# On-chip decay tables and a reordered opening in an attention, feed-forward and expert kernel

## The chip, the cores and the metric

The kernel runs on one core of one Trainium2 chip. The metric is the device time of one execution in microseconds (us). Three runs of the kernel before took 464.21, 465.52 and 466.25 us, with a median of 465.52 us. The engines are TensorE (PE in the profile; PEld is its weight load), VectorE (DVE), ScalarE (ACT), GpSimd (POOL) and SyncE (SP, which here only starts transfers). Each engine works off its own instructions in order and waits on semaphores.

## The reference, cut to what matters

Three steps follow one another: a linear attention with decay, a feed-forward layer, and a routed expert layer. The change touches the attention and the routing.

```python
# attention: 2 batches, 8 heads, 768 positions, head dim 64, blocks of 64; lam is one decay per head
Dmask = where(rel >= 0, lam ** rel, 0.0)              # rel = i - j inside a block
for b in range(nb):
    intra = (qb @ kb.T * Dmask) @ vb
    inter = (qb * lam ** (pos + 1)) @ kv_state        # query powers
    out[:, :, sl] = intra + inter
    kb_dec = kb * lam ** (block - 1 - pos)            # key decays
    kv_state = lam ** block * kv_state + kb_dec.T @ vb
# feed-forward on x = out as (1536, 512): w_in (512, 2048), w_out (2048, 512)
g = where(h > 0, h, exp(min(h, 0)) - 1) with h = x @ w_in;  x = g @ w_out
# experts: rows with x @ w_skip > 0 go to the expert with the largest x @ w_gate
y = gate * (relu(x @ w1[e]) @ w2[e]);  out = x + y on those rows
```

## The kernel before

The 1536 tokens are 12 chunks of 128 (the kernel takes attention blocks of 128, with decay powers to match), six chunks to a batch (CPS) and three to a token block (CPB). For a chunk `c` the attention steps are: `at_scores` (key-query products into two PSUM banks), `at_mask` (VectorE multiplies them by the table `mask`), `at_pv` (TensorE multiplies by the values), `at_qd` (GpSimd multiplies the queries by the power table `lp`), `at_inter` (TensorE adds queries times `state`), `at_kdec` (GpSimd multiplies the keys by the last column of `mask`), `at_kv` (key-value products), `at_decay` (GpSimd scales `state`) and `at_state` (VectorE adds the new products). `at_evac_hi` and `at_evac_lo` split the result from PSUM into a high and a low part, `xT`, for products in three passes.

The tables come from `lam` by way of memory: VectorE makes the powers of each head in `z8` (8 rows), a transfer writes them to `z_dr` in device memory, and transfers from there spread them: `mask` with overlapping rows, and `lp` in two halves. These transfers stand in SP's queue ahead of the keys and values of chunks 0 to 2.

The feed-forward layer has 16 slices `f` of the weights. They arrive as 64-bit floats in 1 MB transfers (`load_ff`), which ScalarE and VectorE convert: `conv_v`, three integer steps `conv_bits`, `conv_hi` (ScalarE) and `conv_lo` (VectorE). `ff1_mm`, `ff1_act`, `ff1_elu`, `ff1_lo` and `ff2` are the layer for one slice and one token block; `LAG` (3) such steps run mixed with chunks 3 to 5, and after them the steps run two ahead. The order of all instructions from the first products on is the order in which the code is written (`manual_schedule`); every engine takes its own share of that order.

At the start ten dummy products of `warm` stand between the scores of chunks 0 to 2, after the first four. Later, `route_pick` and `route_send` of each chunk are put into the steps by the dictionaries `A` (after `ff1_mm`) and `B` (between the second and third `ff2`). `route_rank` is a small product of counts, and `route_send` calls it together with what follows from it.

## Time and profile before

| what | value |
| --- | --- |
| median of three runs | 465.52 us |
| the profiled execution's own time | 463.39 us |
| its span, first to last instruction | 461.3 us |
| TensorE busy | 444.2 us, 96% of the span |
| VectorE busy | 293.1 us, 64% |
| ScalarE busy | 235.2 us, 51% |
| GpSimd busy | 82.8 us, 18% |

The shares are means over stages with different limits. The profiled execution has 2.09 us outside its span. Times within a row count from the start of the span. Where a row ends in brackets, the engine was idle for that long before it, and the name behind the arrow is what ended the wait. A busy TensorE is one with matmuls in flight; it is not by that alone at its fastest.

### The profile page before, as it was taken

To read this page: it belongs to the slowest core of one execution; us is meant where nothing else is said; L and a number is where in the kernel's file an instruction comes from. 1 tells how busy PE (TensorE), PEld (TensorE's weight loads), DVE (VectorE), ACT (ScalarE), POOL (GpSimd) and SP (SyncE) were. 2 spreads that over 40 slices of the span, in tenths; PEclk is the share of its full clock that TensorE was granted. 3 is DMA by queue.
4 is the path that set the end of the run, shared out by engine and by line. 5 is a ranking of instruction groups with operands and counts; after the bars stand their busy time and mean duration, and the time that the engine had idled before them with its cause. 6 is when DMAs were issued, how large, how long until landed. Compare 5 with 4: busy or idle time off the path is not lost.

```text
span 461.3 us, 6824 instructions
## 1 busy us (share of the span) xinstructions
PE 444.2 (96%) x2596; PEld 389.6 (84%) x2596; DVE 293.1 (64%) x558; ACT 235.2 (51%) x378; POOL 82.8 (18%) x106
## 2 busy tenths in 40 slices
PE   8698999999999999999999999999999999999993
PEld 7587899899988888998888898899989788888882
DVE  3789999999622365345244223775546688999970
ACT  2234576776444322443233335465652688888850
POOL 1654002020100124102232000220002112222101
PEclk9999999999999999999999999999999999999998
DMA  6999994604101212210020006334338689999400
GB/s 246 394 416 409 319 123 89 264 1 143 40 1 68 93 35 92 91 70 23 11 91 1 1 0 251 115 105 165 132 136 308 213 313 395 364 366 372 185 18 34
DMA packets 26650, 74.91 MB, mean 162 GB/s; under 512 B 4050, under 2 KB 9690, under 8 KB 24560
## 3 DMA queue, kind: packets, MB, share of 16 engines
q1 hardware_dynamic: 24576, 69.26, 42.4%
q0 software_dynamic: 1600, 3.03, 1.7%
q10 hardware_dynamic: 432, 2.10, 1.2%
q8 instruction: 22, 0.36, 0.3%
q14 instruction: 20, 0.16, 0.1%
HBM read 66.09 MB, written 10.51 MB: 166 GB/s over the span
## 4 chain that ended last, share of the span: by engine, by line
PE 81%; issue 6%; POOL 4%; DVE 4%; DMA 2%; ACT 1%; SPq 0%; POOLq 0%; ACTq 0%; DVEq 0%
PE h L352 28%; PE y L388 21%; PE h L892 8%; PE aux L388 7%; PE y L917 6%; POOL state L314 1%; PE aux L443 1%; DMA lp<-z_dr 1%; PE aux L903 1%; PE aux L280 1%; PE aux L428 1%; PE aux L269 1%; PE y L269 1%; DVE wa L113 1%; DMA z_dr<-z 1%
## 5 line engine op out<-in xcount | busy, mean ns | idle before, releaser
L352 PE MATMUL h<-xT,wa 128*128 128x384 f32 x480 | 91.1, 338 | 1.2 <-DVE xT L293 1.2
L352 PEld LDWEIGHTS h<-xT,wa 128*128 128x128 f32 x480 | 84.7, 188 | 4.7 <-DVE xT L293 1.4
L388 PE MATMUL y<-wa,g 128*128 128x512 f32 x270 | 70.2, 400 | 0.0
L367 ACT ACTIVATE g<-e 128x384 fp32r<-128x384 f32 x64 | 33.4, 523 | 53.4 <-DVE e L364 53.3
L358 ACT ACTIVATE e<-h 128x384 f32<-128x384 f32 x64 | 31.2, 488 | 56.5 <-PE h L352 56.4
L364 DVE SCALAR_TENSOR_TENSOR e<-e,h 128x384 f32<-128x384 f32 x64 | 35.1, 548 | 34.1 <-ACT e L359 34.1
L388 PEld LDWEIGHTS y<-wa,g 128*128 128x128 f32 x270 | 49.0, 188 | 8.9
L352 PE MATMUL h<-xT,wb 128*128 128x384 f32 x288 | 54.2, 336 | 0.0
L352 PEld LDWEIGHTS h<-xT,wb 128*128 128x128 f32 x288 | 50.9, 188 | 2.0
L372 DVE TENSOR_TENSOR g<-e,g 128x384 fp32r<-128x384 f32 x64 | 37.3, 582 | 16.0 <-ACT g L367 16.0
L388 PE MATMUL y<-wb,g 128*128 128x512 f32 x162 | 40.3, 394 | 0.0
L523 POOL DMA_INDIRECT xe<-x,idx x12 | 12.2, 1015 | 148.8 <-DVE xgT L420 49.8
L892 PE MATMUL h<-wa,xgT 128*128 128x512 f32 x144 | 36.1, 397 | 0.1
L388 PEld LDWEIGHTS y<-wb,g 128*128 128x128 f32 x162 | 30.1, 188 | 5.5
L359 ACT ACTIVATE e<-e 128x384 f32<-128x384 f32 x64 | 33.6, 526 | 2.0
L892 PEld LDWEIGHTS h<-wa,xgT 128*128 128x128 f32 x144 | 26.5, 188 | 5.7 <-ACT xgT L419 0.3
L113 DVE TENSOR_TENSOR wa<-big,wa 128x1024 fp32r<-128x1024 f32 x22 | 26.6, 1234 | 4.3 <-ACT wa L112 4.1
L917 PE MATMUL y<-wa,ht 128*128 128x512 f32 x96 | 23.8, 398 | 0.0
L113 DVE TENSOR_TENSOR wa<-ahead,wa 128x1024 fp32r<-128x1024 f32 x18 | 21.6, 1246 | 2.9 <-ACT wa L112 2.7
L112 ACT ACTIVATE wa<-big 128x1024 fp32r<-128x1024 f32 x22 | 22.4, 1056 | 1.2 <-DMA big<-in_wex_dram 1.2
L388 PE MATMUL aux<-wa,g 128*128 128x512 f32 x90 | 23.0, 399 | 0.0
L926 POOL TENSOR_TENSOR o<-o,xg 128x512 f32<-128x512 f32 x7 | 9.1, 1299 | 71.4 <-ACT o L925 71.4
(199 smaller groups left out, 687.4 us busy)
## 6 DMA issues: line engine op xcount, KB each, us to landing
big<-in_wex_dram SPq DMA_DIRECT2D x17, 1024.0 KB, 5.8
ahead<-in_wex_dram SPq DMA_DIRECT2D x15, 1024.0 KB, 6.9
wb<-in_wff_dram SPq DMA_DIRECT2D x10, 1024.0 KB, 13.0
big<-in_wff_dram SPq DMA_DIRECT2D x5, 1024.0 KB, 7.3
big<-in_kq_dram SPq DMA_DIRECT2D x6, 512.0 KB, 3.2
big<-in_kv_dram SPq DMA_DIRECT2D x6, 512.0 KB, 4.2
out_dram<-x SPq DMA_DIRECT2D x12, 256.0 KB, 2.2
xg<-xe SPq DMA_DIRECT2D x8, 257.0 KB, 5.4
```

Of the source, the lines that this page charges most:

```text
L112: nc.scalar.activation(out=w[:, 0, cs], in_=src, func=ACTF.Copy)
L113: nc.vector.tensor_tensor(out=w[:, 1, cs], in0=src, in1=w[:, 0, cs].bitcast(F32), op=ALU.subtract)
L352: nc.tensor.matmul(out=h, lhsT=w[:, wi, k * P:(k + 1) * P], rhs=xT[b][:, xi, k, :], start=(k == 0 and i == 0), stop=(k == 3 and i == 2))
L358: nc.scalar.activation(out=e, in_=h, func=ACTF.Relu, scale=-1.0)
L359: nc.scalar.activation(out=e, in_=e, func=ACTF.Exp, scale=-1.0)
L364: nc.vector.scalar_tensor_tensor(out=e, in0=e, scalar=-1.0, in1=h_t.pop(n), op0=ALU.add, op1=ALU.max)
L367: nc.scalar.activation(out=g[:, 0, :], in_=e, func=ACTF.Copy)
L372: nc.vector.tensor_tensor(out=g[:, 1, :], in0=e_t.pop(n), in1=g[:, 0, :].bitcast(F32), op=ALU.subtract)
L388: nc.tensor.matmul(out=y_t[b, t], lhsT=g[:, gi, t * P:(t + 1) * P], rhs=w[:, wi, 512:1024], start=(f == 0 and i == 0), stop=(f == NF - 1 a ...
L523: sc = nc.gpsimd.indirect_dma_start(out=xe[:, :], out_offset=bass.IndirectOffsetOnAxis(ap=idx[:, c:c + 1], axis=0), in_=x2[:, :], in_offse ...
L892: nc.tensor.matmul(out=h, lhsT=xgT_t[e][:, xi, k * P:(k + 1) * P], rhs=w_t[NF + 8 * e + k][:, wi, j * 512:(j + 1) * 512], start=(i == 0), ...
L917: nc.tensor.matmul(out=y, lhsT=ht[:, hi, k, :], rhs=w_t[NF + 8 * e + 4 + k // 2][:, wi, (k % 2) * 512:(k % 2) * 512 + 512], start=(i == 0) ...
```

## The change

Key decays and query powers no longer come from device memory. TensorE transposes `z8` into a bank that VectorE copies to a new small table `kd` (128 by 8), and multiplies `z8` by a selection matrix `sel` (8 rows of zeros and ones, made by GpSimd) into a bank that ScalarE copies to `lp`. `mask` still goes by way of `z_dr`. The ScalarE queue starts five transfers where it started three. In the opening, the scores of chunk 2, the state of chunk 0 (now copied by ScalarE) and the state product of chunk 1 are written in another order, and ten of the fourteen dummy products go. `at_kv` makes eight products of 64 by 64 in two column halves of the array where it made four of 128 by 128. The first `ff1_mm` takes its products by pass and not by slice. `route_rank` moves behind the third `ff2`, `route_slot` to the step after, `route_send` one step later.

```diff
     gates = const.tile([P, NCH, 2], F32, name="gates")
     mask = mid.tile([P, H, P], F32, name="mask")
     lp = mid.tile([P, 4, P], F32, name="lp")
+    kd = mid.tile([P, H, 1], F32, name="kd")
     state = mid.tile([P, 4, P], F32, name="state")
 
     raw_q = {}
...
         if c % CPS != CPS - 1:
             k3 = kv_t[c][:, 0, :].rearrange("p (h d) -> p h d", h=H)
             nc.gpsimd.tensor_tensor(
-                out=k3, in0=k3, in1=mask[:, :, P - 1:P].to_broadcast([P, H, D]), op=ALU.mult
+                out=k3, in0=k3, in1=kd.to_broadcast([P, H, D]), op=ALU.mult
             )
...
     def at_pv(c, b=None):
-        o = b if b is not None else aux()
-        o_t[c] = o
+        first = c not in o_t
+        if first:
+            o_t[c] = b if b is not None else aux()
+        o = o_t[c]
         v = kv_t[c]
         for hp in range(4):
             cs = slice(hp * P, (hp + 1) * P)
...
                 h = 2 * hp + j
                 nc.tensor.matmul(
                     out=o[64 * j:64 * j + 64, cs], lhsT=v[:, 1, h * D:(h + 1) * D],
-                    rhs=pm_t[c, j][:, hp, :], start=(hp == 0), stop=(c % CPS == 0),
+                    rhs=pm_t[c, j][:, hp, :], start=(first and hp == 0),
+                    stop=(not first or c % CPS == 0),
                     skip_group_check=True,
...
 
-    def at_inter(c):
+    def at_inter(c, b=None):
         if c % CPS:
             qd = qd_t.pop(c)
+            first = c not in o_t
+            if first:
+                o_t[c] = b if b is not None else aux()
             for hp in range(4):
                 nc.tensor.matmul(out=o_t[c][:, hp * P:(hp + 1) * P], lhsT=state[:, hp, :],
-                                 rhs=qd[:, hp, :], start=False, stop=True, skip_group_check=True)
+                                 rhs=qd[:, hp, :], start=(first and hp == 0), stop=not first,
+                                 skip_group_check=True)
 
     def at_evac_hi(c):
         b, cc = divmod(c, CPB)
...
             return
         s = aux()
         t = kv_t[c]
-        for hp in range(4):
-            cs = slice(hp * P, (hp + 1) * P)
-            nc.tensor.matmul(out=s[:, cs], lhsT=t[:, 0, cs], rhs=t[:, 1, cs],
-                             start=True, stop=True)
+        for h in range(H):
+            r = slice(64 * (h % 2), 64 * (h % 2) + 64)
+            cs = slice(h * D, (h + 1) * D)
+            nc.tensor.matmul(out=s[r, cs], lhsT=t[:, 0, cs], rhs=t[:, 1, cs],
+                             start=True, stop=True, skip_group_check=True)
         s_t[c] = s.rearrange("p (k e) -> p k e", k=4)
 
     def at_decay(c):
...
         s3 = s_t.pop(c)
         for j in range(2):
             r = slice(64 * j, 64 * j + 64)
-            if c % CPS == 0:
+            if c == 0:
+                nc.scalar.activation(out=state[r, :, r], in_=s3[r, :, r], func=ACTF.Copy)
+            elif c % CPS == 0:
                 nc.vector.tensor_copy(out=state[r, :, r], in_=s3[r, :, r])
             else:
                 nc.vector.tensor_tensor(out=state[r, :, r], in0=s3[r, :, r],
...
         b, f = where(n)
         h = bank("h", 2)[:, 0:TB]
         w = w_t[f]
-        for k in range(4):
-            for i, (wi, xi) in enumerate(PASSES):
-                nc.tensor.matmul(out=h, lhsT=w[:, wi, k * P:(k + 1) * P], rhs=xT[b][:, xi, k, :],
-                                 start=(k == 0 and i == 0), stop=(k == 3 and i == 2))
+        turns = [(k, i) for k in range(4) for i in range(3)]
+        if n == 0:
+            turns = [(k, i) for i in range(3) for k in range(4)]
+        for j, (k, i) in enumerate(turns):
+            wi, xi = PASSES[i]
+            nc.tensor.matmul(out=h, lhsT=w[:, wi, k * P:(k + 1) * P], rhs=xT[b][:, xi, k, :],
+                             start=(j == 0), stop=(j == 11))
         h_t[n] = h
     def ff1_act(n):
         h = h_t[n]
...
     oh_t = {}
 
     def route_send(c):
-        route_rank(c)
-        route_exp(c)
-        route_slot(c)
         route_gate(c)
         route_out(c)
 
...
         alloc_chunk(1)
         alloc_chunk(2)
         z8 = ph[0].tile([H, ZW], F32, tag="v", name="z8", bufs=2)
+        sel = t2()[0:H]
         nc.sync.dma_start(out=z8[:, P + 1:P + 2], in_=lam.rearrange("(h o) -> h o", o=1))
+        load_ff(0, nc.scalar)
+        dma_kv(0, nc.scalar)
         dma_kq(0, nc.scalar)
-        load_ff(0, nc.scalar)
         dma_kq(1, nc.scalar)
+        dma_kv(1, nc.scalar)
         nc.vector.memset(z8[:, 0:P], 0.0)
         nc.vector.memset(z8[:, P:P + 1], 1.0)
         nc.vector.memset(zrow, 0.0)
+        nc.gpsimd.memset(sel, 0.0)
+        nc.gpsimd.affine_select(out=sel.rearrange("h k (j i) -> h k j i", j=2),
+                                in_=sel.rearrange("h k (j i) -> h k j i", j=2),
+                                pattern=[[-2, 4], [-1, 2], [0, 64]], compare_op=ALU.not_equal,
+                                fill=1.0, base=0, channel_multiplier=1)
+        make_identity(nc, ident)
         nc.gpsimd.memset(blank1[:, 0:1], 0.0)
         nc.gpsimd.memset(blank1[:, 1:2], 4096.0)
         n = 1
...
         with tc.issue_after(zw.ins):
             mr = nc.sync.dma_start(out=mask, in_=toep)
         with tc.issue_after(mr.ins):
-            dma_kv(0)
-            for j in range(2):
-                rows = bass.AP(tensor=zt.tensor, offset=zt.offset + j * ZW + P + 1,
-                               ap=[[0, 64], [2 * ZW, 4], [1, P]])
-                nc.sync.dma_start(out=lp[64 * j:64 * j + 64], in_=rows)
             dma_kq(2)
-            for c in range(1, CPB):
-                dma_kv(c)
+            dma_kv(2)
             load_ff(1)
             for c in range(CPB, CPS):
                 alloc_chunk(c)
...
                 dma_kv(c)
                 load_ff(c - 1)
 
-        make_identity(nc, ident)
         nc.gpsimd.memset(ones, 1.0)
         nc.gpsimd.affine_select(out=ustrict, in_=ones, pattern=[[1, P]], compare_op=ALU.is_gt,
                                 fill=0.0, base=0, channel_multiplier=-1)
...
                 nc.tensor.matmul(out=b[:, 0:P], lhsT=zrow[:, 0:P], rhs=zrow[:, 0:P],
                                  start=True, stop=True)
 
-        sb = [[bank("h", 2), bank("h", 2)], [bank("y", 3), bank("y", 3)],
-              [bank("y", 3), aux()]]
+        sb = [[bank("h", 2), bank("h", 2)], [bank("y", 3), bank("y", 3)]]
         warm(sb[0][0], WARM[0])
+        lpb, kdb = aux(), aux()
+        nc.tensor.transpose(out=kdb[:, 0:H], in_=z8[:, P:2 * P], identity=ident[0:H, 0:H])
+        for k in range(4):
+            nc.tensor.matmul(out=lpb[:, k * P:(k + 1) * P], lhsT=sel[:, k, :],
+                             rhs=z8[:, P + 1:2 * P + 1], start=True, stop=True)
+        nc.vector.tensor_copy(out=kd, in_=kdb[:, 0:H].rearrange("p (h o) -> p h o", o=1))
+        at_kdec(0)
+        conv_v(0)
+        nc.scalar.activation(out=lp, in_=lpb.rearrange("p (k i) -> p k i", k=4), func=ACTF.Copy)
+        at_qd(1)
+        at_kdec(1)
+        pm1 = ph[0].tile([P, 2, 4, P], F32, tag="v", name="pm1", bufs=2)
+        for i in range(3):
+            conv_bits(0, i)
         at_scores(0, sb[0])
-        warm(sb[1][0], WARM[1])
+        at_kv(0)
+        at_state(0)
+        conv_hi(0)
         at_scores(1, sb[1])
-        warm(sb[2][0], WARM[2])
-        at_qd(1)
-        conv_v(0)
-        pm1 = ph[0].tile([P, 2, 4, P], F32, tag="v", name="pm1", bufs=2)
-        conv_bits(0, 0)
-        conv_bits(0, 1)
-        for c in range(2):
-            for half in range(2):
-                at_mask(c, half, pm1[:, half] if c else None)
-            at_kdec(c)
-            if c == 0:
-                conv_bits(0, 2)
-                conv_hi(0)
+        at_inter(1, bank("y", 3))
+        at_decay(1)
+        at_qd(2)
+        at_kdec(2)
+        at_kv(1)
+        for half in range(2):
+            at_mask(0, half)
+        for half in range(2):
+            at_mask(1, half, pm1[:, half])
+        at_pv(0)
+        at_state(1)
+        at_evac_hi(0)
+        at_scores(2, [bank("h", 2), bank("h", 2)])
+        at_evac_lo(0)
+        at_pv(1)
+        at_evac_hi(1)
+        for half in range(2):
+            at_mask(2, half)
+        at_inter(2)
+        at_decay(2)
+        at_evac_lo(1)
+        at_pv(2)
+        at_evac_hi(2)
         conv_lo(0)
-        for c in range(CPB):
-            at_pv(c, bank("y", 3) if c == 1 else None)
-            if c == 0:
-                at_scores(2, sb[2])
-                for half in range(2):
-                    at_mask(2, half)
-                at_qd(2)
-                at_kdec(2)
-            at_inter(c)
-            at_decay(c)
-            at_kv(c)
-            at_evac_hi(c)
-            if c == 1:
-                conv_v(1)
-            at_state(c)
-            at_evac_lo(c)
-            if c == 1:
-                conv_bits(1, 0)
-                conv_bits(1, 1)
+        at_evac_lo(2)
+        conv_v(1)
+        at_kv(2)
+        at_state(2)
+        conv_bits(1, 0)
+        conv_bits(1, 1)
         for f in range(CPS - 1, 10):
             load_ff(f)
         at_scores(CPB, [bank("y", 3), bank("y", 3)])
...
         N = NBLK * NF
         LAST = NBLK - 1
         TAIL = 3
-        A, B, C = {}, {}, {}
+        A, B, C, Y, Z = {}, {}, {}, {}, {}
         early = None
 
         def at_S(c):
...
             for i in range(CPB):
                 put(B, n + i, route_T, c0 + i)
                 put(A, n + 1 + i, route_pick, c0 + i)
-                put(B, n + 1 + i, route_send, c0 + i)
+                put(B, n + 1 + i, route_exp, c0 + i)
+                put(Z, n + 1 + i, route_rank, c0 + i)
+                put(Y, n + 2 + i, route_slot, c0 + i)
+                put(B, n + 2 + i, route_send, c0 + i)
 
         for i in range(CPB):
             put(A, J + 2 * i + 1, at_P, CPS + i)
...
             b, f = where(n)
             ff1_elu(n + 1)
             ff1_mm(n + 2)
-            for g, a in A.pop(n, []):
+            for g, a in Y.pop(n, []) + A.pop(n, []):
                 g(*a)
             ff1_lo(n + 1)
             for g, a in C.pop(n, []):
...
             for g, a in B.pop(n, []):
                 g(*a)
             ff2(n, 2)
+            for g, a in Z.pop(n, []):
+                g(*a)
             if f == NF - 1:
                 for t in range(CPB):
                     evac_y(b, t)
...
         route_slot(last[2])
         route_gate(last[2])
         route_out(last[2])
-        assert not A
+        assert not A and not B and not Y and not Z
```

ScalarE's queue, from its first instruction (`wb<-in_kq_dram` are the keys and queries of a chunk, `wb<-in_kv_dram` its keys and values by position, `big<-in_wff_dram` the weights of slice 0; ACT_TABLE_LOAD fetches the function table). Before:

```order
L203 DMA wb<-in_kq_dram 128x1024
L124 DMA big<-in_wff_dram 128x2048
L203 DMA wb<-in_kq_dram 128x1024
L134 ACT_TABLE_LOAD
L134 ACTIVATE v<-big 128x1024
```

And in the change:

```order
L125 DMA big<-in_wff_dram 128x2048
L207 DMA wb<-in_kv_dram 128x1024
L204 DMA wb<-in_kq_dram 128x1024 x2
L207 DMA wb<-in_kv_dram 128x1024 [waits DMAHW0_49]
L135 ACT_TABLE_LOAD
L135 ACTIVATE v<-big 128x1024
L640 ACTIVATE lp<-aux 128x512 [waits PE_49]
```

The weights now stand first, two transfers of keys and values are added, and the second of them waits for the weights' landing with the table load behind it.

VectorE, from the first table use to the second slice's conversion (`t` and `pm` are masked scores, `v<-big,v` a step of `conv_bits`, `wa<-v,wa` is `conv_lo`, `xT` the low parts). Before:

```order
L149 SCALAR_TENSOR_TENSOR v<-big,v 128x1024
L232 TENSOR_TENSOR t_211<-h,mask 128x512
L232 TENSOR_TENSOR t_213<-h,mask 128x512
L152 SCALAR_TENSOR_TENSOR v<-big,v 128x1024
L232 TENSOR_TENSOR pm_208<-y,mask 128x512 x2
L163 TENSOR_TENSOR wa<-v,wa 128x1024
L232 TENSOR_TENSOR t_240<-y,mask 128x512
L232 TENSOR_TENSOR t_242<-aux,mask 128x512
L325 COPY state<-aux 64x4x64 x2
L293 TENSOR_TENSOR xT<-aux,xT 128x4x128
L327 TENSOR_TENSOR state<-aux,state 64x4x64 x2
L293 TENSOR_TENSOR xT<-y,xT 128x4x128
```

And in the change:

```order
L150 SCALAR_TENSOR_TENSOR v<-big,v 128x1024
L153 SCALAR_TENSOR_TENSOR v<-big,v 128x1024
L233 TENSOR_TENSOR t_247<-h,mask 128x512
L233 TENSOR_TENSOR t_249<-h,mask 128x512
L233 TENSOR_TENSOR pm_195<-y,mask 128x512 x2
L338 TENSOR_TENSOR state<-aux,state 64x4x64 x2
L301 TENSOR_TENSOR xT<-aux,xT 128x4x128
L233 TENSOR_TENSOR t_286<-h,mask 128x512
L233 TENSOR_TENSOR t_288<-h,mask 128x512
L301 TENSOR_TENSOR xT<-y,xT 128x4x128
L164 TENSOR_TENSOR wa<-v,wa 128x1024
L301 TENSOR_TENSOR xT<-aux,xT 128x4x128
```

The last step of `conv_bits` moves ahead of the masks, the copy of `state` leaves VectorE, and the addition to `state` stands ahead of the low parts.

TensorE, its first instructions (`zrow` feeds the dummy products, L222 and L223 are `at_scores`, L315 is `at_kv`, L287 is `at_inter`). Before:

```order
L614 MATMUL h<-zrow 128x128 x4
L222 MATMUL h<-wb 128x128 x8
L614 MATMUL y<-zrow 128x128 x6
L222 MATMUL y<-wb 128x128 x8
L614 MATMUL y<-zrow 128x128 x4
```

And in the change:

```order
L627 MATMUL h<-zrow 128x128 x4
L633 MATMUL aux<-ident,z_109 128x8
L635 MATMUL aux<-z_109,t_110 128x128 x4
L223 MATMUL h<-wb 128x128 x8
L315 MATMUL aux<-wb 64x64 x8
L223 MATMUL y<-wb 128x128 x8
L287 MATMUL y<-g,state 128x128 x4
L315 MATMUL aux<-wb 64x64 x8
```

The dummy products between the scores are gone, and the state path of chunks 0 and 1 stands ahead of the first masked products.

## Rows read from the trace of the kernel before

**Rows 1.** The page's busy times by engine.

```profile
PE 444.2 (96%) x2596; PEld 389.6 (84%) x2596; DVE 293.1 (64%) x558; ACT 235.2 (51%) x378; POOL 82.8 (18%) x106
```

**Rows 2.** Busy time by stretch; columns as in the first line.

```profile
core 0: us, PE busy (x) PEld busy (x) DVE busy (x) ACT busy (x) POOL busy (x), PEclk, DMA share, GB/s
5.00:10.00 5.00, 5.00 (x32) 4.55 (x32) 1.11 (x2) 1.13 (x1) 0.00 (x0) 1.00 0.64 243
...
35.00:40.00 5.00, 3.84 (x27) 2.90 (x29) 4.94 (x8) 2.04 (x3) 1.51 (x2) 1.00 1.04 401
...
80.00:100.00 20.00, 20.00 (x101) 18.02 (x100) 19.90 (x24) 14.70 (x22) 3.13 (x1) 1.00 0.39 155
...
150.00:200.00 50.00, 49.68 (x340) 44.13 (x338) 23.56 (x76) 16.37 (x34) 11.22 (x17) 1.00 0.24 88
```

**Rows 3.** The chain of waits, 0 to 70 us: start, length, what.

```profile
4.34 3.52 DMA z_dr<-z
...
8.96 4.89 DMA lp<-z_dr
...
14.44 1.28 POOL g L249
```

**Rows 4.** Timeline of TensorE, ScalarE and its queue, 0 to 22 us.

```profile
2.19 1.28 ACT L134 ACT_TABLE_LOAD   x1 [2.19 <-issue]
4.17 2.08 PE L222 MATMUL h<-wb 64*128 64x128 f32 x16 [0.83 <-DMA wb<-in_kq_dram]
...
7.69 1.13 ACT L134 ACTIVATE v<-big 128x1024 f32<-128x1024 f32 x1 [4.21 <-DMA big<-in_wff_dram]
...
9.03 1.40 PEld L222 LDWEIGHTS y<-wb 64*128 64x128 f32 x16 [0.23 <-DMA wb<-in_kq_dram]
...
21.96 1.16 ACT L134 ACTIVATE v<-big 128x1024 f32<-128x1024 f32 x1 [0.28 <-DMA big<-in_wff_dram]
```

**Rows 5.** Transfer rate in 40 slices of 1.75 us, 0 to 70 us.

```profile
GB/s 0 321 400 403 80 223 360 290 410 435 412 386 426 424 398 426 433 389 438 381 379 407 421 431 407 431 426 403 431 389 245 229 134 77 155 144 135 125 62 183
```

**Rows 6.** Timeline of VectorE, 11 to 29 us.

```profile
11.86 1.29 DVE L232 TENSOR_TENSOR t<-h,mask 128x512 f32<-128x512 f32 x2 [1.05 <-DMA mask<-z_dr]
13.06 1.22 DVE L152 SCALAR_TENSOR_TENSOR v<-big,v 128x1024 int32<-128x1024 int32 x1
...
15.40 1.40 DVE L163 TENSOR_TENSOR wa<-v,wa 128x1024 fp32r<-128x1024 f32 x1
...
18.96 0.88 DVE L325 COPY state<-aux 64x256 f32<-64x256 f32 x2 [0.81 <-PE aux L306]
19.87 0.69 DVE L293 TENSOR_TENSOR xT<-aux,xT 128x512 fp32r<-128x512 f32 x1
22.05 0.91 DVE L327 TENSOR_TENSOR state<-aux,state 64x256 f32<-64x256 f32 x2 [1.49 <-PE aux L306]
...
23.60 0.68 DVE L146 TENSOR_SCALAR v<-v 128x1024 int32<-128x1024 int32 x1
24.32 1.64 DVE L149 SCALAR_TENSOR_TENSOR v<-big,v 128x1024 int32<-128x1024 int32 x1
...
27.54 1.28 DVE L232 TENSOR_TENSOR t<-y,mask 128x512 f32<-128x512 f32 x2
```

**Rows 7.** Timeline of TensorE, four places between 6 and 174 us.

```profile
6.18 2.93 PE L614 MATMUL y<-zrow 128*128 128x128 f32 x12
...
10.56 1.16 PE L614 MATMUL y<-zrow 128*128 128x128 f32 x8
...
27.68 2.18 PE L352 MATMUL h<-xT,wa 128*128 128x384 f32 x11 [1.15 <-DVE xT L293]
...
153.83 1.09 PE L269 MATMUL y<-t,big 128*64 128x128 f32 x16
154.86 1.16 PE L306 MATMUL y<-big 128*128 128x128 f32 x8
...
173.06 0.17 PE L481 MATMUL y<-pick,ustrict 128*128 128x8 bf16 x1 [0.32 <-DVE pick L462]
```

## The prediction, made blind

> **What bounds the kernel now.** I read the busy times first, then the stretches, then the chain of waits, and then the timelines of the first 30 us. TensorE is busy for 444.2 of 461.3 us [rows 1], so only about 17 us hold no matmul. The stretches tell where: from 80 to 100 us TensorE is busy for 20.00 of 20.00 us, and from 150 to 200 us for 49.68 of 50.00, while from 35 to 40 us it has only 3.84 of 5.00 and VectorE has 4.94 [rows 2]. So VectorE sets the pace early, and TensorE sets it later. If the opening gets shorter, both parts move forward as a block. The question is how early the opening ends.
>
> The chain of waits through the opening goes over transfers that spread the tables: 3.52 us to write the powers to memory at 4.34, later 4.89 us for `lp`, and only then 1.28 us of GpSimd for the powered queries at 14.44 [rows 3]. The other table, `mask`, lands at 11.86, where VectorE had been idle for 1.05 us [rows 6]. From there VectorE is the engine to follow, because everything up to the masks of chunk 3 at 27.54 passes through it, 15.68 us later [rows 6].
>
> **The opening, from the landing of the masks.** I count what leaves VectorE's queue between 11.86 and 27.54 [rows 6]. The last step of the first conversion, 1.22 us at 13.06, is now ahead of the masks, in the time in which VectorE waits for them anyway. The copy of the state, 0.88 us at 18.96, goes to ScalarE. The two waits for TensorE's key-value products, 0.81 and 1.49 us, should go: those products wait for the keys that GpSimd scales, the keys no longer wait for `mask`, and the products now stand ahead of the first masked products. Together that is 1.22 + 0.88 + 0.81 + 1.49 = 4.40 us.
>
> The same from the other side: what stays on VectorE from the masks' landing is three pairs of masks (3 x 1.29), two additions to the state (2 x 0.91), three low parts (3 x 0.69), `conv_lo` (1.40) and two steps for slice 1 (0.68 and 1.64), 11.48 us [rows 6]. Against 15.68 that saves 4.20; neighbouring instructions overlap by some hundredths, so 4.40 may stand.
>
> Would a new wait take its place? With matmul groups of about 1.1 us [rows 7] and 0.69 for ScalarE's high part (VectorE's price for the same shape, [rows 6]), chunk 1's masked products end about 1.29 + 3 x 1.1 = 4.6 us after the landing and its high part at 5.3. VectorE wants that high part after 3 x 1.29 + 0.91 + 0.69 = 5.47. The cover is about 0.2 us, so this hides as long as TensorE runs at its later rate. I charge 0.3 us for ties of this kind. Behind such a wait stand `conv_lo`, the low parts and the whole conversion of slice 1, so it would go straight into the end time.
>
> **When the masks land.** ScalarE's queue now carries 3 MB where it carried 2. Before, the weights (1.5 MB into that queue) were there at 7.69 and the last keys (2 MB) at 9.03 [rows 4], that is 1.34 us per half MB. So the last of the new transfers comes at about 9.03 + 2 x 1.34 = 11.7. The write of the powers and the transfer of `mask` share the transfer engines with it. The lowest cost is nothing, if the small transfers get their turn at once: the write already ran beside a loaded queue before. The highest is all of the added traffic, 2.7 us. The rate fell to 80 GB/s in the slice from 7 to 8.75 us [rows 5], and the added bytes fill that hole first, at no cost to anyone. What then still runs beside `mask` is less than 1 MB; I take 1.0 us, nearer to the low end.
>
> The table load of 1.28 us at 2.19 [rows 4] was hidden. Now it stands behind a transfer that waits for slice 0's weights, so it is exposed. The weights come first in the queue and so about 1.3 us earlier than 7.69; load and gain cancel, and the conversion starts where it did. VectorE's three conversion steps then end at about 7.69 + 1.13 + 0.68 + 2 x 1.22 = 11.9, just as the masks come. In SP's queue the keys of chunk 2 now stand right behind `mask`, so they land one step of 1.34 us after it, and TensorE wants them 1.29 + 1.1 = 2.4 us after it.
>
> **The weights of slice 1.** ScalarE starts on them at 21.96, after waiting 0.28 us for their transfer [rows 4], so this transfer is late next. The stream loses the transfer of `lp`, a quarter of a MB (about 0.7 us at the step above), and fills the hole of 80 GB/s, 1.4 us at the neighbours' 400 [rows 5]. It comes at about 19.8, its first conversion pass (1.16) is done at 21.0, and VectorE gets to it at 11.86 + 1.0 + 9.2 = 22.1. That hides it by 1.1 us.
>
> **The rest of the opening.** The spreading products (a transpose and four matmuls) and GpSimd's two instructions for `sel` lie where TensorE and GpSimd have nothing else. The removed dummy products lay in such time too. The order of passes in the first `ff1_mm` lets four of its products start on high parts alone; before, it waited 1.15 us for the last low part [rows 7], and since VectorE and not this product is the end of the chain, I count nothing. From slice 1's conversion on, VectorE's queue is the same as before, so the gain is carried to the dense part of TensorE.
>
> **The later parts.** The rank product's wait of 0.32 us at 173.06 [rows 7] should go, since it now has a third `ff2` ahead of it; TensorE's busy 49.68 of 50.00 shows that there is no more to win [rows 2]. `route_slot` now makes VectorE wait for that product one step later, and the low part queued behind it is wanted only a step after that; VectorE has 23.56 of 50.00 us of work there [rows 2], so this hides. The key-value products have no row in their new shape. The nearest is the masked product's, also 16 records on 64 columns of weights: 1.09 us against 1.16 for the present group of 8 [rows 7]. If the halved moving side counts in full it is 0.55. If each change of shape costs what the rows can't show, I allow 0.2 us more than now. Five such groups lie in the dense part: from +3.0 to -1.0 us. I take the nearest row, 5 x 0.07 = 0.3.
>
> The Trainium skill (TensorEngine Tiling, Key Properties) says that a change of the tiling mode drains TensorE, and the new shape adds such a change on both sides of a group. The present switch from masked to full products, 153.83 to 154.86, takes less than the group's own 1.09 us, so this trace shows no drain worth naming. By the rule alone this term would be a loss.
>
> **Sum.** 4.40 - 0.3 - 1.0 + 0.32 + 0.3 = 3.7 us off. The profiled execution took 463.39 us (461.3 in the span, 2.09 around it) and becomes 459.7; it is 2.13 under the median of the runs, 465.52, which becomes 461.8. I give that.
>
> **Rivals.** *The transfers bind.* The powers' write or `mask` gets no turn until ScalarE's queue is empty, 2.7 us late, or slice 1's weights still land near 21.9. For it: the write took 3.52 us for a few KB beside a loaded queue [rows 3], and slice 1 is waited for already. Against it: that write did come through before the last keys. Then 4.40 - 0.3 - 2.7 + 0.6 = 2.0 us stay: 463.5.
>
> *The slow clock (slower).* Before, 12 records at 6.18 took 2.93 us, 244 ns each, and 8 at 10.56 took 1.16, 145 ns each [rows 7]; the groups of scores at 4.17 and 9.03 differ likewise [rows 4]. TensorE went to about twice its rate near 9 us, after it had worked almost without a break from 4.17 on. The granted clock reads 1.00, the level of 2.4 GHz, over all of 5 to 10 us [rows 2], so here the durations tell more than that column. The change takes ten dummy products away and leaves TensorE with nothing between the spreading products and the first scores, whose keys come as the third transfer, at about 9.0. The Trainium skill (TensorE: Matmul & The Clock Gate, Part 1) calls the slow level the default and says that sustained work releases it; the doubling agrees. From 9.0 there are 12 groups before the first `ff1_mm`: at 1.1 us each and 2.2 for that product it ends at 24.4, at 2.08 each and 4.4 at 38.4. Before, it ended at 29.86 [rows 7]. So this path decides from the sixth group at the slow rate on, and if all are slow the kernel loses 8.5 us: 465.5 + 8.5 - 0.6 = 473.4. Against it: from 9.0 on these groups follow one another closely, as those did that raised the rate before.
>
> *It doesn't matter.* If VectorE's waits merely move to its next inputs, only the 0.6 us of the later parts stay: 464.9. Against it: from 35 to 40 us VectorE is busy for 4.94 of 5.00 us, so it hardly waits for inputs there [rows 2].
>
> **Chances.** The forecast 0.66, the transfers 0.18, the slow clock 0.09, no matter 0.07. Changes under 0.5% (2.3 us) can't be told from none. Of the forecast 0.63 is faster and 0.03 the same, of the transfers 0.08 and 0.10, of the slow clock 0.08 is slower and 0.01 the same, and the last is the same. That makes 0.71 faster, 0.21 the same, 0.08 slower. The low end is a mask that lands on time with key-value products half-way to their best (4.4 + 0.3 + 1.8 = 6.5 off, 459.0). The high end is the last rival, 465.0; beyond it lies the slow clock.
>
> **What would show it.** Right: VectorE starts the masks at 12 to 13.5 us and those of chunk 3 at 23 to 24; the first `ff1_mm` ends near 24 to 25; the chain enters TensorE's dense part about 4 us sooner. Wrong: masks after 14, slice 1's conversion waiting for its transfer, groups of 16 records at 2 us beyond 15 us, or a key-value group of more than 1.3 us. The prediction fails if VectorE waits again between the first masks and chunk 3's.

## The result and the profile after

The changed kernel takes 460.25 us (median of 6 runs, 459.71 to 462.12), the kernel before, beside it, 464.88 us (6 runs, 463.68 to 466.25). The ratio is 0.9905, with a 95% interval from 0.9878 to 0.9933. The forecast was 461.8 us in a range from 459.0 to 465.0. The profiled execution took 460.44 us, span 458.4; that is 2.95 us under the profiled execution of before, where 3.7 were forecast.

The busy times on the page of after, against [rows 1]:

```profile
PE 442.1 (96%) x2665; PEld 385.0 (84%) x2665; DVE 295.0 (64%) x557; ACT 236.0 (51%) x381; POOL 86.2 (19%) x108
```

TensorE is busy for 2.1 us less. The transfer rate, 0 to 70 us, as in [rows 5]:

```profile
GB/s 0 225 407 417 414 371 260 367 442 414 405 442 405 410 433 407 414 424 356 409 421 417 421 431 417 417 417 304 351 272 182 118 107 150 146 134 112 61 101 220
```

The hole in the fifth slice (80 GB/s) is filled: 414.

Busy time by stretch of after, columns as in [rows 2]:

```profile
36.00:38.00 2.00, 2.00 (x6) 1.52 (x5) 2.00 (x4) 0.00 (x1) 0.00 (x0) 0.50 1.02 426
...
150.00:200.00 50.00, 50.00 (x373) 44.23 (x371) 23.55 (x74) 16.81 (x36) 11.11 (x17) 1.00 0.24 87
```

TensorE's last gap between 150 and 200 us is gone (49.68 before). But the granted clock (the last column but two) fell to 0.50, the level of 1.2 GHz, from 36 to 38 us; before, it read 1.00 there.

The queues and ScalarE of after, timeline (start, length, what); they answer to [rows 3, 4]:

```profile
4.67 0.29 SPq L579 DMA_DIRECT2D z_dr<-z  x1
8.84 0.40 SPq L583 DMA_DIRECT2D mask<-z_dr  x1
...
6.11 1.28 ACT L135 ACT_TABLE_LOAD   x1 [6.11 <-DMA big<-in_wff_dram]
...
20.33 1.14 ACT L135 ACTIVATE v<-big 128x1024 f32<-128x1024 f32 x1
```

The transfers of `lp` are gone from SyncE's queue. The table load is exposed, as forecast, and the weights of slice 1 are there before ScalarE wants them, at 20.33.

VectorE of after, against [rows 6]:

```profile
2.17 2.48 DVE L576 TENSOR_SCALAR z<-z 8x1 f32<-8x1 f32 x7 [0.96 <-DMA z<-in_lam_dram]
...
13.13 1.29 DVE L233 TENSOR_TENSOR t<-h,mask 128x512 f32<-128x512 f32 x2 [0.41 <-DMA mask<-z_dr]
...
22.97 1.95 DVE L150 SCALAR_TENSOR_TENSOR v<-big,v 128x1024 int32<-128x1024 int32 x1
24.95 1.29 DVE L233 TENSOR_TENSOR t<-y,mask 128x512 f32<-128x512 f32 x2
```

The masks of chunk 3 start at 24.95 us instead of 27.54, 2.59 sooner. VectorE waits for nothing between the first masks and these: the way from one to the other is 11.82 us long, where it was 15.68. TensorE of after, against [rows 4, 7]:

```profile
8.33 2.08 PE L223 MATMUL h<-wb 64*128 64x128 f32 x16 [1.44 <-DMA wb<-in_kq_dram]
...
11.39 1.20 PE L223 MATMUL y<-wb 64*128 64x128 f32 x16
...
21.95 2.35 PE L366 MATMUL h<-xT,wa 128*128 128x384 f32 x12
25.70 0.43 PE L272 MATMUL aux<-t,wa 128*64 128x128 f32 x2 [1.40 <-DVE t L233]
...
33.92 1.13 PE L223 MATMUL aux<-wa 64*128 64x128 f32 x14 [1.72 <-DVE state L338]
34.98 3.87 PE L402 MATMUL y<-wa,g 128*128 128x512 f32 x9
...
151.08 1.09 PE L272 MATMUL y<-t,big 128*64 128x128 f32 x16
...
157.30 0.95 PE L457 MATMUL y<-wg,t 128*128 128x9 f32 x8
...
165.26 1.16 PE L287 MATMUL y<-t,state 128*128 128x128 f32 x8
166.35 0.69 PE L315 MATMUL y<-big 128*64 128x64 f32 x16
166.96 1.06 PE L457 MATMUL y<-wg,t 128*128 128x9 f32 x8
167.88 1.64 PE L402 MATMUL aux<-wb,g 128*128 128x512 f32 x6
...
170.54 0.17 PE L492 MATMUL y<-pick,ustrict 128*128 128x8 bf16 x1
```

Only one group of scores runs at the slow rate, 2.08 us at 8.33. The group at 34.98 takes 3.87 us for work that took 2.34 before, while the granted clock is low; TensorE had waited 1.40 and 1.72 us before that.

Where the 2.9 us of span come from, by the start of the same TensorE group in both traces: at the dense part 1.94 (53.51 against 55.45), from there to the masked products of chunk 6 another 0.81, from those to the first expert product 0.10, and behind it 0.05. The 0.81 isn't the change's doing, and the 0.10 hides two effects that nearly cancel; both are taken up below, with the second execution of before.

### The profile page after: what moved, and what is told of

It is laid out like the page before. It is cut to its first block, busy times and chain, and to the rows that moved or that the text cites. A ratio compares the mean times of both kernels' runs of the same rounds, so it can differ in the third digit from the quotient of the medians.

```text
span 458.4 us, 6973 instructions
## 1 busy us (share of the span) xinstructions
PE 442.1 (96%) x2665; PEld 385.0 (84%) x2665; DVE 295.0 (64%) x557; ACT 236.0 (51%) x381; POOL 86.2 (19%) x108
## 4 chain that ended last, share of the span: by engine, by line
PE 86%; issue 4%; DVE 4%; ACT 2%; DMA 1%; POOL 1%; ACTq 0%; POOLq 0%
PE h L366 29%; PE y L402 23%; PE h L922 8%; PE aux L402 8%; PE y L947 6%; DMA wb<-in_kq_dram 1%; PE aux L457 1%; PE aux L223 1%; PE aux L287 1%; PE aux L272 1%; PE aux L933 1%; PE y L223 1%; DVE wa L114 1%; PE aux L442 1%; PE y L287 1%
## 5 line engine op out<-in xcount | busy, mean ns | idle before, releaser
L366 PEld LDWEIGHTS h<-xT,wa 128*128 128x128 f32 x480 | 83.7, 188 | 3.6 <-DVE wa L164 0.7
L402 PE MATMUL y<-wa,g 128*128 128x512 f32 x270 | 71.7, 407 | 0.0
L402 PEld LDWEIGHTS y<-wa,g 128*128 128x128 f32 x270 | 50.0, 191 | 9.8
```

The source lines that it names most:

```text
L366: nc.tensor.matmul(out=h, lhsT=w[:, wi, k * P:(k + 1) * P], rhs=xT[b][:, xi, k, :], start=(j == 0), stop=(j == 11))
L402: nc.tensor.matmul(out=y_t[b, t], lhsT=g[:, gi, t * P:(t + 1) * P], rhs=w[:, wi, 512:1024], start=(f == 0 and i == 0), stop=(f == NF - 1 a ...
```

## Experiments

Times are medians beside runs of the kernel before on the same chip, which took 464.13, 463.68 and 464.20 us in the three sets.

**The old key-value products.** `kv_undone` is the changed kernel with the four products of before in `at_kv`.

```diff
-        for h in range(H):
-            ...
+        for hp in range(4):
+            cs = slice(hp * P, (hp + 1) * P)
+            nc.tensor.matmul(out=s[:, cs], lhsT=t[:, 0, cs], rhs=t[:, 1, cs], start=True, stop=True)
```

> The change with its key-value products back in four full 128 by 128 products. If the halved moving side is what pays (groups of 0.6 us in the change against 0.9 to 1.0 before), each of the five groups in the dense part loses 0.35 to 0.4 us and the kernel is 1.8 us slower than the change, near 462.0 against 460.3, so about 2.8 us under the kernel before. If the forecast's nearest row was right, the groups are worth 0.3 us together and nothing can be told from the change.

Measured: 462.38 us, ratio 0.9973 [0.9952, 0.9994], span 460.1. Taking the new shape away costs 1.7 to 2.1 us by the medians (the changed kernel's two are 460.25 and 460.69) and 1.3 to 1.7 in the profiled spans. Of the spans' difference 0.82 lies between the masked products of chunk 6 and the first expert product; 0.4 to 0.7 is there already when the dense part begins (54.22 against 53.80 and 53.51). Its rows for chunks 6 and 7:

```profile
151.75 1.09 PE L272 MATMUL y<-t,big 128*64 128x128 f32 x16
...
158.39 0.95 PE L456 MATMUL y<-wg,t 128*128 128x9 f32 x8
...
166.35 1.16 PE L287 MATMUL y<-t,state 128*128 128x128 f32 x8
167.34 1.07 PE L314 MATMUL y<-big 128*128 128x128 f32 x8
168.25 0.96 PE L456 MATMUL y<-wg,t 128*128 128x9 f32 x8
169.07 1.17 PE L401 MATMUL aux<-wb,g 128*128 128x512 f32 x4
```

Read start to start, the three steps from the state product of chunk 7 on take 0.99, 0.91 and 0.82 us with the old shape, 1.09, 0.61 and 0.92 with the new. The group gains 0.30, and the step ahead of it and the step behind it each lose 0.10. Where the group stands right behind masked products, which use the array in 64 columns too, there is no such loss ahead: in chunk 6 the stretch from the masked products to the next logits gains 0.42 (6.64 us in `kv_undone`, 6.22 in after).

**The rank product put back.** `rank_undone` puts `route_rank`, `route_exp` and `route_slot` back into `route_send`.

```diff
+        route_rank(c)
+        route_exp(c)
+        route_slot(c)
         route_gate(c)
...
-                put(B, n + 1 + i, route_exp, c0 + i)
-                put(Z, n + 1 + i, route_rank, c0 + i)
-                put(Y, n + 2 + i, route_slot, c0 + i)
-                put(B, n + 2 + i, route_send, c0 + i)
+                put(B, n + 1 + i, route_send, c0 + i)
```

> The change with route_rank, route_exp and route_slot back in route_send. If the move only takes away the one wait seen before, this is 0.3 us slower than the change (460.6), which can't be told from it, and TensorE shows one wait for pick of about 0.3 us near 170 us. The rival, that the move is a main part of the gain because it also spares the second and third feed-forward products an interruption, would make it 1 us or more slower.

Measured: 460.61 us, 0.9918 [0.9894, 0.9942], span 458.9. TensorE's wait is back:

```profile
170.16 0.17 PE L495 MATMUL y<-pick,ustrict 128*128 128x8 bf16 x1 [0.38 <-DVE pick L476]
```

The stretch that holds it (from the second to the third group of logits in the dense part) takes 6.25 us here and 5.78 in after, so the move is worth 0.47 us in its place. Elsewhere it costs: four other steps from one group of logits to the next take 5.64 to 5.67 us in after and 5.60 to 5.63 here, and over the whole way from chunk 6 to the first expert product 0.17 us of gain is left (199.86 against 200.03). Against the other kernels' medians it can't be told from nothing.

**The opening alone.** `opening_only` undoes both, so that only the new opening stays.

```diff
+        for hp in range(4):   # at_kv as before
...
+                put(B, n + 1 + i, route_send, c0 + i)   # as before
```

> The change with both the key-value products and the rank product as before: only the opening is new. If the opening's lead at the start of the dense part (1.9 us in the profile of the change) is carried to the end, this is 2 us under the kernel before, near 462.6. If the opening's lead is lost later (the dense part waits for weights that have not come any earlier), it is within 0.5 us of the kernel before. If the opening is worth the forecast's 3.1 us, it is near 461.5.

Measured: 463.01 us, 0.9976 [0.9956, 0.9995], span 461.4. The mask landed at 14.01 us, 2.15 later than before, and the dense part began 0.86 us sooner. Of that the profiled execution gave 0.64 back in one new wait of TensorE:

```profile
187.12 2.20 PE L365 MATMUL h<-xT,wa 128*128 128x384 f32 x11 [0.64 <-DVE xT L301]
```

From chunk 6 to the first expert product this kernel takes 201.67 us where before took 199.96. The wait is 0.64 of these 1.71 us; the other 1.07 go with a slower pace of the dense products, shown below. So the new opening by itself brings about 1 us by the medians, not 3.1.

**The new products alone.** `kv_alone` is the kernel before with the new loop in `at_kv`.

```diff
-        for hp in range(4):
+        for h in range(H):
+            r = slice(64 * (h % 2), 64 * (h % 2) + 64)
...
+            nc.tensor.matmul(out=s[r, cs], lhsT=t[:, 0, cs], rhs=t[:, 1, cs], ...)
```

> The kernel before with nothing but the key-value products in eight 64 by 64 products. If each group falls from 0.9 to 1.0 us to 0.6, the five groups of the dense part save 1.8 us and the kernel is near 0.996 of the kernel before, with the opening's groups (off VectorE's path) worth little. If the forecast's 0.3 us holds, it is 0.999 and can't be told from it.

Measured: 463.89 us, 1.0004 [0.9978, 1.003], though the profiled execution, the fastest of 12, took 461.66 (span 459.7). Its row from 10 to 20 us has a granted clock of 0.83:

```profile
10.00:20.00 10.00, 6.37 (x76) 5.39 (x74) 7.51 (x11) 1.54 (x2) 5.68 (x5) 0.83 1.02 374
```

The mean granted clock of its 12 runs is 0.988, of 59 runs of the kernel before 0.990. A straight line through the 59 (time against mean clock, correlation -0.79) gives 0.29 us for each 0.001. By that line the runs of `kv_alone` lose some 0.6 us to the clock. In its trace the way from chunk 6 to the first expert product takes 199.47 us, 0.49 less than before. The rest of the contrast to `kv_undone` stays open: put into the kernel before, the new products show no gain in the medians.

**The same kernels again.** `change_again`, `before_again` and `kv_alone_again` are unaltered second profiles, so there is no edit to show.

> The changed kernel itself, unaltered, beside the three others, so that they can be compared with it on the same chip: 0.990 of the kernel before, and again a fall of the granted clock for some 3 us between 28 and 40 us if the two waits of TensorE there cause it.

Measured: 460.69 us (7 runs), 0.9934 [0.991, 0.9958], span 458.8. The mask came at 13.74 us and the masks of chunk 3 started at 25.88; the clock fell from 28 to 31 us in place of 35 to 39, and the dense part began at 53.80. So the opening's gain in a second execution is 1.65 us at the dense part.

> The kernel before, unaltered, profiled a second time. Open: in its first profile the x12 groups of ff1 followed each other at 2.12 us in the first half of the dense part and at 2.08 us after, and the dense part to pv(0) took 98.4 us, against 96.9 to 97.6 us in the kernels of this study. Theory A, the pace belongs to the execution: it differs from 98.4 us by 0.3 us or more here. Theory B, it belongs to the kernel (where its groups lie): 98.3 to 98.5 us again, with groups of 2.12 us until about 148 us.

> The kernel before with the key-value products in 128x64 tiles alone, profiled a second time. Theory A, the pace belongs to the execution: the dense part to pv(0), 96.9 us in its first profile, comes out 0.3 us or more away from it. Theory B, it belongs to the kernel: 96.8 to 97.1 us and a span of 459.6 to 459.8 us again.

Measured: 467.82 us (span 465.8) and 465.12 us (span 463.1), in one run each. Theory A holds for both. For `before_again`, the busy times of two stretches, and two consecutive groups of `ff1_mm`:

```profile
15.00:20.00 5.00, 3.90 (x24) 3.56 (x24) 3.49 (x5) 1.04 (x2) 5.00 (x4) 0.57 1.04 419
...
350.00:355.00 5.00, 5.00 (x30) 4.88 (x30) 2.17 (x11) 0.00 (x0) 0.00 (x0) 0.52 1.02 419
```

```profile
80.78 2.25 PE L352 MATMUL h<-xT,wa 128*128 128x384 f32 x12
84.92 2.25 PE L352 MATMUL h<-xT,wa 128*128 128x384 f32 x12
```

The same groups in the first profile of before, and in after, each with two more from behind chunk 6:

```profile
82.96 2.28 PE L352 MATMUL h<-xT,wa 128*128 128x384 f32 x12
87.17 2.28 PE L352 MATMUL h<-xT,wa 128*128 128x384 f32 x12
...
304.15 2.25 PE L352 MATMUL h<-xT,wa 128*128 128x384 f32 x12
308.30 2.25 PE L352 MATMUL h<-xT,wa 128*128 128x384 f32 x12
```

```profile
80.81 2.25 PE L366 MATMUL h<-xT,wa 128*128 128x384 f32 x12
84.98 2.25 PE L366 MATMUL h<-xT,wa 128*128 128x384 f32 x12
...
305.19 2.25 PE L366 MATMUL h<-xT,wa 128*128 128x384 f32 x12
309.36 2.25 PE L366 MATMUL h<-xT,wa 128*128 128x384 f32 x12
```

Two things differ between executions of one kernel. The clock: at 0.57 and 0.52 in these stretches, it puts the dense part at 57.81 us (2.36 later than in the first profile) and makes the stretch ahead of the first expert product 3.19 us longer (8.35 against 5.16). And the pace of the dense part: up to chunk 6, a pair of `ff1_mm` and `ff2` takes 4.14 us here, 4.21 in the first profile of before, 4.17 in all ten profiles with the new opening. From the dense part to chunk 6 that is 96.94, 98.38 and 97.5 us. So the 0.81 us of this stretch compare a slow pace of before with the middle one.

Behind chunk 6 it is the other way round. There a pair takes 4.15 us in all four profiles with the old opening and 4.17 in all ten with the new, so the pace goes with the opening and not with the execution alone. `opening_only` puts it at 1.07 us up to the first expert product. By the runs that undo them the new key-value products are worth 0.82 us there and the rank product's move 0.17, so about nothing is left, and 0.10 was measured. In which way the new opening holds the pace at 4.17 wasn't found out.

**The clock held up.** `clock_held` adds small products of zeros in the two waits of TensorE that come ahead of the clock's fall.

```diff
+                o = aux()
+                warm(o, 4)              # ahead of at_pv(3)
...
+                    warm(banks[0], 5)   # ahead of at_scores(4)
```

> The change with nine dummy products added where TensorE waits near 24 and 32 us (four before the masked products of chunk 3, five before the scores of chunk 4). If these waits let the clock fall to its lower level at 35 us, the granted clock stays at 1.00 from 30 to 40 us, the first second-layer group takes about 2.35 us and not 3.87, VectorE's two waits for the state near 41 us (0.91 and 0.28) shrink, and the dense part starts 0.6 to 1.2 us earlier: 459.3 to 459.7. The rival: VectorE sets the start of the dense part anyway, so the clock comes back and the time does not move (460.3).

Measured: 460.82 us, 0.9935 [0.991, 0.996], span 457.9. The clock and the group that took 3.87 us:

```profile
36.00:38.00 2.00, 2.00 (x19) 1.45 (x19) 2.00 (x4) 0.00 (x0) 0.00 (x0) 1.00 1.00 414
```

```profile
35.09 2.37 PE L402 MATMUL y<-wa,g 128*128 128x512 f32 x9
```

The fall is gone, and the dense part begins 0.55 us sooner than in after, with first masks at the same time (13.14). From the masks of chunk 3 to the dense part it is 27.91 us here and 27.91 before, but 28.56 in after: the fall had cost 0.65. In `change_again`, where it came from 28 to 31 us, the same way takes 27.92, so there it cost nothing. The median shows nothing of it: 0.5 us is less than these runs can tell.

The waits alone don't decide whether the clock falls. `kv_undone` had waits of 1.44 and 1.73 us in these places and fell as after did; `opening_only`, with 1.44 and 1.72, stayed at 1.00. Where the first wait was 2.05 to 2.08 us (`change_again`, `rank_undone`, `mask_first`) the clock fell soon behind it, from 28 or 31 us on, and in the three kernels with the products of zeros it stayed at 1.00. That these products held it is likely and not shown, since `opening_only` and `keys_act` stayed at 1.00 without them.

**ScalarE for the keys.** `keys_act` scales the keys of chunks 3 and 4 on ScalarE and not on GpSimd; `keys_act_held` does that and has the products of zeros of `clock_held` as well.

```diff
+        if c in (CPB, CPB + 1):
+            for h in range(H):
+                kh = kv_t[c][:, 0, h * D:(h + 1) * D]
+                nc.scalar.activation(out=kh, in_=kh, func=ACTF.Copy, scale=kd[:, h, :])
```

> The change with the key scaling of chunks 3 and 4 on ScalarE (eight small instructions each) in place of GpSimd. If GpSimd's work at the same time is what stretches VectorE's conversion steps (1.95 us at 22.97 in the change against 1.22 elsewhere), the step beside chunk 3's keys takes 1.2 to 1.4 us, the masks of chunk 3 start near 24.3 and not 24.95, and the dense part starts about 0.6 us earlier. The rival: the stretch comes from the transfers landing in memory, and the step stays near 1.9.

> Both at once: key scaling of chunks 3 and 4 on ScalarE, and the nine dummy products that hold the clock. If the two losses are separate, the dense part starts 1.1 to 1.3 us earlier than in the change, near 52.3, and the kernel is near 459.0 (0.988 of the kernel before). If they overlap, it starts where the better one of them does.

Measured: 460.42 us, 0.9925 [0.9896, 0.9954], and 459.86 us, 0.9923 [0.9897, 0.995]; the dense part begins at 52.98 and 52.96. With GpSimd out of the way VectorE's step, 1.95 us in after, has this row in `keys_act`:

```profile
23.82 1.22 DVE L150 SCALAR_TENSOR_TENSOR v<-big,v 128x1024 int32<-128x1024 int32 x1
```

So work of GpSimd beside it had stretched that step by 0.73 us. The clock didn't fall in either kernel, in `keys_act` in spite of waits of 1.35 and 1.71 us. Both edits together begin the dense part no sooner than each alone, but that they take away the same time isn't shown: the first masks started 0.8 us later in these two profiles (13.97 and 13.95) than in `clock_held`, and the way from there to the masks of chunk 3 is shorter by as much (11.11 us against 11.91).

**The mask first.** `mask_first` takes the keys and values of chunk 1 from ScalarE's queue and puts them on SyncE's behind `mask`.

```diff
-        dma_kq(1, nc.scalar)
-        dma_kv(1, nc.scalar)
...
+            dma_kq(1)
+            dma_kv(1)
```

> The changed kernel, with the key and value loads of pair 1 taken from ScalarE's queue and put on SyncE's behind the decay mask. Theory A, the mask is late because a MB more is under way on the other queue: VectorE's first mask step at 12.0 to 12.6 us instead of 13.1 to 13.7, masks of chunk 3 up to 0.8 us sooner, the median 0.3 to 0.8 us below the changed kernel's. Theory B, the mask is late only because the chain ahead of its issue is 0.7 us longer: still at 13.1 us or later, and the time unchanged within 0.3 us, or longer where pair 1's keys now come later than 20.3 us to the first mixing step.

Measured: 464.36 us, 1.0006 [0.998, 1.0032], span 461.4. SyncE's queue, VectorE and TensorE:

```profile
4.68 0.28 SPq L577 DMA_DIRECT2D z_dr<-z  x1
8.19 0.40 SPq L581 DMA_DIRECT2D mask<-z_dr  x1
```

```profile
12.72 1.29 DVE L233 TENSOR_TENSOR t<-h,mask 128x512 f32<-128x512 f32 x2 [1.88 <-DMA mask<-z_dr]
```

```profile
13.92 2.08 PE L223 MATMUL y<-wb 64*128 64x128 f32 x16 [2.57 <-DMA wb<-in_kq_dram]
```

The chain ahead of the write took the same 2.48 us, but from the write's start to that of `mask` it is 3.51 us, as before (3.54), where after has 4.17. The mask was there at 12.72, 0.4 to 1.3 us sooner than in the other profiles with the new opening. So the added MB on the other queue does delay it, by this one profile. The keys of chunk 1 then come too late, TensorE waits 2.57 us for them, and the whole gain of the change is lost.

**A quiet start.** `quiet_start` is `keys_act_held` with GpSimd's constants (`ones`, `ustrict`, `desc`, `base`, `places`, `gates`) built after the first mixed steps.

```diff
-        nc.gpsimd.memset(ones, 1.0)
...
+        late()   # the same lines, called behind the first mixed steps
```

> The changed kernel with the key decay of chunks 3 and 4 on ScalarE and the small products ahead of two groups (both as in the runs before), and with GpSimd's constants built after the first mixing steps, so that GpSimd does little beside VectorE's first chain. Theory A, GpSimd's work stretches VectorE's: the z8 steps together 1.8 to 2.0 us instead of 2.48, the mask issued 0.5 us sooner and its first use at 12.6 us or, with keys_act's 13.9 as the measure, 13.4; the dense part from 52.4 to 52.6 us; median about 459.3 us. Theory B, the chain's length has another cause or the mask step then waits for VectorE's conversions (which end at 12.7 us): the mask step moves by less than 0.2 us and the time not at all.

Measured: 460.00 us, 0.991 [0.9878, 0.9942], span 457.8. VectorE, SyncE's queue, and then TensorE:

```profile
2.23 1.76 DVE L578 TENSOR_SCALAR z<-z 8x1 f32<-8x1 f32 x7 [1.03 <-DMA z<-in_lam_dram]
...
13.29 1.29 DVE L233 TENSOR_TENSOR t<-h,mask 128x512 f32<-128x512 f32 x2 [0.58 <-DMA mask<-z_dr]
...
16.98 0.69 DVE L305 TENSOR_TENSOR xT<-aux,xT 128x512 fp32r<-128x512 f32 x1 [0.25 <-ACT xT L299]
```

```profile
4.03 0.29 SPq L581 DMA_DIRECT2D z_dr<-z  x1
8.77 0.40 SPq L585 DMA_DIRECT2D mask<-z_dr  x1
```

```profile
8.35 2.08 PE L223 MATMUL h<-wb 64*128 64x128 f32 x16 [2.10 <-DMA wb<-in_kq_dram]
```

The first steps take 1.76 us again, and the write starts 0.64 us sooner than in after. But the transfer of `mask` behind it starts at 8.77 us, only 0.07 sooner: the write took 4.74 us in place of 4.17. So the shorter chain gave next to nothing to the mask, and theory A fails there. That the mask is used at 13.29 us, 0.66 sooner than in `keys_act_held` (13.95), comes from the transfer of `mask` itself, and other profiles with the new opening had it as early (13.13 in after).

The dense part begins at 52.88, 0.08 sooner. On the way to the masks of chunk 3 VectorE now waits 0.20, 0.25 and 0.23 us, twice for high parts that follow TensorE's masked products, and TensorE had come to these without a wait from 8.35 us on. So an earlier mask finds TensorE's own work in its way. Neither theory foresaw that. This is no better than the changed kernel within what the medians tell.

## Why the prediction came out right

The direction, the places and the sum held; its terms were off on both sides and made up for each other. That the sum came so near is luck: the opening was to give 3.1 us and gives about 1 by `opening_only`, the key-value products were to give 0.3 and give 1.7 to 2.1 by `kv_undone`. Two of the prediction's own signs of being right did not show: the masks of chunk 3 were to start at 23 to 24 us (24.95), and the dense part about 4 us sooner (1.94).

- **VectorE's path, 4.40 less 0.3.** Measured 15.68 - 11.82 = 3.86 us against 4.10. Both waits went, and in after no wait took their place; the tie that the 0.3 stands for shows in `change_again`, where VectorE waits 0.23 us for the high part of chunk 1 and the path is 12.14. The missing 0.24 lies in steps that took longer than the rows they were priced by, such as slice 1's second step (1.95 us for 1.64). GpSimd stretched that step, by `keys_act`, and the 1.64 was no undisturbed price either: there it takes 1.22.
- **The mask, 1.0 us later.** 1.27 in after, up to 2.15 in `opening_only`. The added traffic is the cause that the runs show: from the write's start to that of `mask` it is 4.17 us, before 3.54, and 3.51 without that traffic (`mask_first`). VectorE's steps for `z8` take 2.48 us for 1.77, beside GpSimd's older constants, which its new instructions push back to this time. The prediction costed that at nothing, and `quiet_start` bears it out so far: without it the mask's transfer starts only 0.07 us sooner. The transfer of `mask` itself took from 4.1 to 5.0 us in the profiles with the new opening, and what sets that is open.
- **From the masks to the dense part.** The prediction carried the gain on unchanged: 3.1 us, of which 2.59 were there at the masks of chunk 3 and 1.94 at the dense part. The 0.65 in between went with the fall of the clock, since `clock_held` has 27.91 us for this way as before. In `change_again` 1.66 us were there at the masks of chunk 3 and 1.65 at the dense part. The prediction looked for a slow clock only before the first `ff1_mm`, not behind it.
- **The transfers as rival.** The mask's delay came half-way to its 2.7 us in after and near it in `opening_only`, but slice 1's weights came in time (20.33, forecast 19.8). The wait that the old kernel had there didn't return.
- **The slow clock as rival.** One group of scores ran at 2.08 us in after, and the first `ff1_mm` ended at 24.3 us, where 24.4 was worked out for TensorE's path. In eight of the ten profiles with the new opening the second group took 1.8 to 2.1 us as well; in `change_again`, one of them, the first `ff1_mm` still ended at 24.55. The rival fell, though its path turned out to be as long as VectorE's.
- **The rank product, 0.32.** The wait is gone; 0.30 us in its stretch against before (6.08 to 5.78), 0.47 by undoing it. What the product costs in its new places leaves 0.17 of this.
- **The key-value products, 0.3.** Five groups in the dense part give 0.82 us by `kv_undone`: 0.4 in chunk 6 and 0.1 in each of the others. Another 0.4 to 0.7 comes in the opening, where the prediction priced them at nothing. The nearest row was the wrong one: it ran 16 records of twice the columns. (The 1.8 of the range's low end is not half-way between its 0.3 and 3.0; that is 1.65.) The Trainium skill (TensorEngine Tiling, Key Properties) has the rule that a change of the tiling mode drains TensorE. The rows above agree with the rule, at a small price: two changes more cost about 0.3 us together, which leaves 0.1 of a gain of 0.4. It does not turn the term into a loss. I had found nothing worth naming in the trace, but it was there: full groups in a row overlap by 0.17 us (166.35 + 1.16 against 167.34 in `kv_undone`), the masked and the full group of [rows 7] by 0.06.
- **No matter, as rival.** It fell: the masks of chunk 3 are 2.59 us sooner.
- **The size.** 2.95 us by the profiled executions, 3.6 by the means (59 runs of before 464.2, 6 and 7 of the changed kernel 460.6 each), 4.6 in the first set. The clock makes part of that spread: 0.990 in the mean over the runs of before, 0.993 and 0.992 in the changed kernel, some 0.6 to 1.0 us by the line above. That is a correlation and not an experiment. The traces fit it: from 10 to 20 us the mean granted clock is 1.00 in all ten profiles with the new opening, and 1.00, 0.78, 0.83 and 0.74 in the four with the old. So three of four executions with the old opening had a lower clock there, which the first profile of before, and the forecast made from it, don't show.

Not tried by itself: the state's copy on ScalarE, the order of passes in the first `ff1_mm`, the dummy products taken out. What sets the pace of the dense part stays open.

## What to carry to other kernels

A gain in an opening is worth what arrives at the first engine that never waits again; follow it to there, through every other chain that ties with it, before it is summed. When a small transfer that gates a chain gets a new MB beside it on another queue, or a step of VectorE gets GpSimd beside it, give that a price, and read from the next link of the chain whether it arrives there. Profile both kernels twice before a difference under one per cent is put down to a row.

## What the hardware showed unexpectedly

- GpSimd beside VectorE: 1.95 us for a step that takes 1.22 without it (`keys_act`), and 2.48 us for seven steps on 8 numbers that take 1.76 (`quiet_start`).
- An 8 KB write, counted to the start of the transfer that waits for it, took 3.5 to 3.9 us beside 2 MB on the other queue (five profiles) and 4.1 to 4.7 beside 3 MB (nine).
- The granted clock fell to the 1.2 GHz level after short waits in the opening (1.40 and 1.72 us in after), not in the same place in two executions of one kernel, and not at all in `opening_only` with the same waits. With products of zeros in the two waits it stayed at 1.00 in three profiles.
- With the clock granted at 1.00 all the time, pairs of the same products ran at three paces, 4.14, 4.17 and 4.21 us a pair.
- Switching between full and 64-column products costs some 0.15 us a change, an estimate from the gains of 0.42 us without and 0.10 with two more changes.
